# Attention values in two scaled float16 parts instead of three bfloat16 parts, from the second batch on

## The chip, the core and the metric

The kernel runs on one core of a Trainium2 chip. The metric is the device time of one execution in microseconds. Five engines work side by side: TensorE (PE in the profile, with its weight loads as PEld), VectorE (DVE), ScalarE (ACT), GpSimd (POOL) and SyncE (SP), which here issues every DMA.

## The reference

Inputs are q, k and v of shape (4, 8, 768, 64): 4 batches, 8 heads, 768 tokens, 64 numbers a head. The output of the attention goes through a mixture of four experts that all see every token.

```python
k_sum = k.reshape(B, H, nb, 32, D).max(axis=3)       # nb = 24 blocks
v_sum = v.reshape(B, H, nb, 32, D).mean(axis=3)
scores_l = scale * q @ k.T        # kept only where |i - j| < 16
scores_s = scale * q @ k_sum.T + log(32)
a = softmax(concat([scores_l, scores_s]))
attn = a @ concat([v, v_sum])     # (B, H, S, D) -> x of (3072, 512)
p = domain_probs / (domain_probs.sum(-1, keepdims=True) + 1e-9)
for e in range(4):
    h = np.maximum(x @ w1[e], 0.0)            # 512 -> 1024
    out += p[:, e:e+1] * (h @ w2[e])          # 1024 -> 512
```

## The kernel before

**Pieces.** The attention is cut into 64 pieces. Piece n handles batch n // 16, the 96 queries number (n // 2) % 8, and four heads (n % 2 says which four). For its 96 queries it needs 128 neighbouring keys (a window) and 24 block summaries. Pieces 0 to 7 are done by a separate function in the first 40 us (`first_tokens`); pieces 8 to 63 go through the steps below.

**Steps of a piece.** `load_piece` loads k (tile `kr`) and q with v (tile `qv`). `stage_a` splits them into parts of lower precision, since products are formed from parts whose sum is the full number: `ks` and `qs` as float32r parts for the scores, and v as three bfloat16 parts (`v12` holds the first two, `v3` the third), made by ACT, POOL, ACT and POOL in turn. `scores` forms the score matrix (PSUM tile `psc`), the maxima on DVE and the exponentials on ACT (tile `ms`). `probs` scales by the row sum (`rs`) and writes the weights as two float16 parts into tile `aw`; the weights of the 24 summaries are stored there as five blocks of 24 columns (`a5`: three copies of the high part, two of the rest). `transposed` turns `aw` by a DMA transpose into `awT`. `values` multiplies: for each of 4 heads, v1·hi, v1·lo, v2·hi, v2·lo, v3·hi and the summaries, thus 6 matmuls of 96 columns a head and 24 a piece, into PSUM tile `px`. Two heads at a time use the left and the right 64 columns of the array. `to_x` scales px away by 1/ASC; from piece 16 on it goes to DRAM (`xs`, `xd`) and comes back later as `xr`.

**Once per batch.** `setup_k` loads k in four chunks of 128x768 (`kch`) and takes block maxima. `setup_v` loads v likewise (`vch`), takes block sums, and `stack_v` and `split_v` make of them the summary operand `vs`: 4 transposes (`pvs`), a copy, and 8 instructions on DVE that split it into bfloat16 parts. All chunks share two buffers (tag "chunk"), so the third load waits until the first chunk has been reduced.

**The experts.** Tokens go through the experts in blocks of 384, the last six blocks in three pairs. The first product gives PSUM tiles `ph`, or `pha` to `phd` for the pairs (a seven-product scheme); `to_h` splits the result into `hh` and `hl`; the second product gives `po`, which DVE adds into `acc`. Weights arrive as `wr`, are split into high and low parts and are stored split in DRAM (`wd`, `wds`) for the later blocks.

**What sets the order.** The function writes a list `steps` of (place, step, piece), and `advance` puts steps between the matmuls of the experts by place. The setup of batch b stands two places (k) and half a place or one place (v) ahead of its first piece; a place is one piece. Up to the eighth place, the program order is kept; from there on a scheduler with a timeline of its own orders the instructions of each engine, apart from the chunk loads, which stay in program order. Every engine works its list in order, and SP's list is one queue: a DMA that must wait holds all DMAs behind it.

Of the kernel before, what the change touches and what calls it, by code (L numbers as in the profile page):

```python
# [21 lines left out]
QB = 96  # L22
# [40 lines left out]
def attn_moe(ctx: ExitStack, tc: tile.TileContext, qvL, qv0, v0L, kD, kT, vT, w1L, w2L, dpL, cst, out):  # L63
# [46 lines left out]
    def mixing():  # L110
        SP.dma_start(pw, dpL)
        s = const.tile([P, NT, 1], F32, name="dps")
        V.tensor_reduce(s, pw, axis=AX.X, op=ALU.add)
        V.tensor_scalar_add(s, s, EPS)
        V.reciprocal(s, s)
        V.tensor_tensor(pw, pw, s.broadcast_to([P, NT, E]), op=ALU.mult)


    per = 2 * (TB // QB)
    aw_bufs = {}  # L120

# [19 lines left out]
    def load_chunk(b, hp, ch, src):  # L141
        tc.keep_in_program_order(
            nc.sync.dma_start(ch, src[b, 2 * hp : 2 * hp + 2].rearrange("h d s -> (h d) s"))
        )
# [4 lines left out]
    def chunk(name):  # L149
        return sb.tile([P, S], F32, name=name, tag="chunk", bufs=CHUNKS)  # L150
# [17 lines left out]
    def setup_v(b):  # L168
# [4 lines left out]
            block_stats(ch, vsr, hp, ALU.add)  # L173
        stack_v(b, vsr)

    def stack_v(b, vsr):
        vs5 = sb.tile([P, G, 5, NB], F32, name=f"vs5_{b}", tag="chunk", bufs=CHUNKS)
        A.mul(vs5, vsr.rearrange("p h (o n) -> p h o n", o=1).broadcast_to([P, G, 5, NB]), 1.0 / BLK)
        pt = ps_av.tile([P, 512], F32, name=f"pvs{b}", tag="av")
        for hp in range(G):  # L180
            PE.transpose(
                pt[:NST, hp * P : (hp + 1) * P],
                vs5[:, hp].rearrange("p o n -> p (o n)"),
                ident,
            )
        v0 = sb.tile([NST, 512], F32, name=f"v0_{b}", tag="chunk", bufs=CHUNKS)
        A.copy(v0, pt[:NST, :])
        split_v(b, v0)

    def split_v(b, v0):  # L190
        b12 = sb.tile([NST, 2, 512], BF16, name=f"b12_{b}", tag="awT", bufs=2)
        b1, b2 = b12[:, 0, :], b12[:, 1, :]
        V.tensor_copy(b1, v0)
        V.tensor_tensor(v0, v0, b1, op=ALU.subtract)
        V.tensor_copy(b2, v0)
        V.tensor_tensor(v0, v0, b2, op=ALU.subtract)
        V.tensor_scalar_mul(b1, b1, gsel[0])
# [21 lines left out]
    def stage_a(n):  # L219
        b, i, g = n // 16, (n // 2) % NQ, n % 2  # L220
        h0 = g * G
        t = st[n]
        qr = t["qv"][:, 0 : G * QB].rearrange("p (h s) -> p h s", s=QB)
        vr = t["qv"][:, G * QB :].rearrange("p (h d) -> p h d", d=D)
        kr = t["kr"]
        PL.tensor_copy(kr[:, :, KW:KA], ksum[b][:, h0 : h0 + G, :])
        ks = []
        tag, bufs = ("x", NX) if spare_x(n) else ("kl", 2)
        for half in range(2):
            k2 = sb.tile([P, 2, 2, KA], F32R, name=f"ks{n}_{half}", tag=tag, bufs=bufs)  # L230
# [12 lines left out]
        PL.tensor_tensor(v3, vr, v12[:, :, 1, :], op=ALU.subtract)
        t.update(ks=ks, qs=qs, v=(v12, v3))
# [33 lines left out]
    def probs(n):  # L278
        ms, rs = st[n]["ms"], st[n]["rs"]
        aw = aw_of(n)  # L280
        V.tensor_scalar(rs, rs, EPS, 1.0 / ASC, op0=ALU.add, op1=ALU.mult)
        V.reciprocal(rs, rs)
        V.tensor_tensor(
            ms, ms, rs.rearrange("p (h o) -> p h o", o=1).broadcast_to([QB, G, KA]), op=ALU.mult
        )
        A.copy(aw[:, 0:G, :], ms[:, :, 0:KW])
        V.tensor_tensor(aw[:, G : 2 * G, :], ms[:, :, 0:KW], aw[:, 0:G, :], op=ALU.subtract)
        sm = ms[:, :, KW:KA]
        a5 = aw[:, 2 * G : 3 * G, 0:NST].rearrange("p h (o n) -> p h o n", n=NB)
        sm = sm.rearrange("p h (o n) -> p h o n", o=1)  # L290
        A.copy(a5[:, :, 0:3, :], sm.broadcast_to([QB, G, 3, NB]))
        V.tensor_tensor(
            a5[:, :, 3:5, :], sm.broadcast_to([QB, G, 2, NB]), a5[:, :, 0:2, :], op=ALU.subtract
        )
# [7 lines left out]
    def values(n):  # L302
        b, g = n // 16, n % 2
        t = st[n]
        awT, (v12, v3), vs = t["awT"], t["v"], vsum[b]
        if g == 0:
            t["bank"] = ps_av.tile([P, 512], F32, name=f"px{n}", tag="av")
        else:
            t["bank"] = st[n - 1]["bank"]
        px = t["px"] = t["bank"][:, g * 2 * QB : (g + 1) * 2 * QB].rearrange("p (c q) -> p c q", q=QB)  # L310
        for c in range(2):
            terms = []
            for j in (2 * c, 2 * c + 1):
                hi, lo, su = awT[:, j, :], awT[:, G + j, :], awT[:NST, 2 * G + j, :]
# [10 lines left out]
            for m in range(6):  # L325
                for o in range(2):
                    PE.matmul(px[o * D : (o + 1) * D, c, :], *terms[o][m], start=m == 0, stop=m == 5)

    def both_values(n):
        values(n - 1)  # L330
# [8 lines left out]
    def to_x(n):  # L339
        i = (n // 2) % NQ  # L340
        tb, ib = n // per, i % (TB // QB)
        pair = [st.pop(m)["px"] for m in (n - 1, n)]
        if tb < 2:
            if tb not in xT:
                xT[tb] = x_block(tb)
            parts = [[x[:, :, ib * QB : (ib + 1) * QB] for x in xT[tb][g]] for g in range(2)]
            for g in range(2):
                A.mul(parts[g][0], pair[g], 1.0 / ASC)
            for g in range(2):
                V.scalar_tensor_tensor(  # L350
                    parts[g][1], pair[g], 1.0 / ASC, parts[g][0].bitcast(F32), op0=ALU.mult, op1=ALU.subtract
                )
            return
        xs = sb.tile([P, 2, 2, QB], F32, name=f"xs{n}", tag="xt")
        A.mul(xs[:, 0], pair[0], 1.0 / ASC)
        A.mul(xs[:, 1], pair[1], 1.0 / ASC)
        if (tb // 2, ib) not in xraw:
            xraw[tb // 2, ib] = dram.tile([P, 4, 2, QB], F32, name=f"xd{tb // 2}_{ib}")
        SP.dma_start(xraw[tb // 2, ib][:, tb % 2 : 4 : 2], xs)
        written[tb // 2, ib] = written.get((tb // 2, ib), 0) + 2  # L360
# [685 lines left out]
```

## Time and profile before

| | us |
|---|---|
| median of 3 runs (1173.69 to 1174.64) | 1174.48 |
| the profiled execution | 1176.52 |
| its span, first to last instruction | 1174.7 |
| PE busy | 1150.5 (98%) |
| DVE busy | 631.4 (54%) |
| ACT busy | 541.2 (46%) |
| POOL busy | 468.5 (40%) |

The profiled execution took 1.8 us more than its span and 2.0 us more than the median of the runs. In the list of stretches, each engine stands with its busy time and the number of its instructions in brackets, followed by the clock that was granted to PE (1.00 is full), the busy share of the DMA engines, and the rate. In the chain of work that ended last, each row is start, length and what was done. A group row ends with its count, its busy time and the mean of one in ns, then the idle time ahead of it.

### The profile page before, as it was taken

The page shows a single profiled execution, that of the slowest core. Times are in us where ns is not written, and L with a number is a line of the kernel's source. Part 1 is how long each engine was busy: PE and PEld are TensorE (multiplying, and loading weights), DVE is VectorE, ACT ScalarE, POOL GpSimd, SP SyncE. Part 2 cuts the span into 40 slices and gives each one's busy share as a digit, 9 for nine tenths or more (in the row PEclk, how much of TensorE's full clock was granted, in tenths as well). Part 3 has the DMA queues.
Part 4 walks back from the last instruction along what each step waited for, and adds up shares of the span by engine and source line. Part 5 has one row for each costly group of instructions (what it writes and reads, how often), then busy time and mean ns, then how long its engine had stood idle before and what let it go on. Part 6 is the DMA issues. An engine that isn't in the chain of part 4 may idle for free.

```text
span 1174.7 us, 20612 instructions
## 1 busy us (share of the span) xinstructions
PE 1150.5 (98%) x7188; PEld 1021.0 (87%) x7188; DVE 631.4 (54%) x1519; ACT 541.2 (46%) x1586; POOL 468.5 (40%) x578
## 2 busy tenths in 40 slices
PE   9898899999979999999999999999999999999998
PEld 7787789998968989898898989889898998989896
DVE  6778775555796837558586543535354222323131
ACT  5678667655666736546375443434343211202020
POOL 2398677846786737547265122221202000000000
PEclk9999999999999999999999999999999999999999
DMA  6699787957996878789963859678571556566531
GB/s 240 227 281 321 225 250 218 305 118 215 307 251 182 272 228 263 225 277 288 320 196 102 255 149 289 202 213 284 141 205 61 159 156 212 165 197 189 163 98 54
DMA packets 202329, 249.66 MB, mean 213 GB/s; under 512 B 82672, under 2 KB 118512, under 8 KB 202224
## 3 DMA queue, kind: packets, MB, share of 16 engines
q1 hardware_dynamic: 202224, 248.34, 69.6%
q8 instruction: 57, 0.93, 0.3%
q14 instruction: 48, 0.39, 0.1%
HBM read 174.22 MB, written 57.15 MB: 197 GB/s over the span
## 4 chain that ended last, share of the span: by engine, by line
PE 85%; DMA 4%; DVE 4%; POOL 3%; ACT 2%; issue 1%; SPq 1%; POOLq 0%; DVEq 0%; ACTq 0%
PE po L75 42%; PE phb L75 13%; PE pha L75 9%; PE ph L75 5%; PE phd L75 4%; PE phc L75 4%; PE psc L75 4%; PE px L75 3%; DMA vch<-in_vT 1%; PE pav L75 1%; DMA wr<-in_w2L 1%; DMA kch<-in_kT 1%; DVE ms L75 1%; SPq L75 1%; ACT ms L75 1%
## 5 line engine op out<-in xcount | busy, mean ns | idle before, releaser
L75 PE MATMUL po<-w,hh 128*128 128x512 f32 x1536 | 480.5, 394 | 0.0
L75 PEld LDWEIGHTS po<-w,hh 128*128 128x128 f32 x1536 | 284.2, 188 | 61.0
L75 PE MATMUL po<-w,hl 128*128 128x512 f32 x768 | 302.8, 397 | 0.0
L75 PEld LDWEIGHTS po<-w,hl 128*128 128x128 f32 x768 | 144.4, 188 | 31.5
L75 POOL TENSOR_TENSOR ks<-kr,ks 128x304 fp32r<-128x304 f32 x112 | 99.7, 897 | 176.8 <-ACT ks L75 160.5
L75 DVE CUSTOM_DVE_ANT_0 ms<-psc,c_sb 96x152 f32<-96x152 f32 x256 | 69.2, 306 | 104.6 <-PE psc L75 103.4
L75 PE MATMUL phb<-xh_t,w1s 128*128 128x384 f32 x384 | 114.2, 338 | 0.1
L75 ACT ACTIVATE ms<-ms,nb 96x152 f32<-96x152 f32 x256 | 104.3, 415 | 16.5 <-DVE nb L75 15.6
L75 PE MATMUL pha<-xh,w 128*128 128x384 f32 x384 | 110.7, 335 | 0.0
L75 DVE SCALAR_TENSOR_TENSOR acc<-po,pw,acc 128x512 f32<-128x512 f32 x72 | 51.9, 746 | 108.8 <-PE po L75 108.8
L75 PE MATMUL ph<-xh,wh 128*128 128x384 f32 x256 | 88.0, 347 | 4.8 <-ACT wh L75 3.7
L75 PE MATMUL ph<-xl,wh 128*128 128x384 f32 x256 | 87.4, 341 | 2.3 <-DVE xl L75 2.3
L75 DVE TENSOR_TENSOR aw<-ms,aw 96x512 f16<-96x512 f32 x112 | 77.2, 723 | 21.5 <-ACT aw L75 21.3
L75 PE MATMUL ph<-xh,wl 128*128 128x384 f32 x256 | 87.1, 341 | 1.2 <-POOL wl L75 1.2
L75 ACT CAST ks<-kr 128x304 fp32r<-128x304 f32 x112 | 48.1, 445 | 80.4 <-PE psc L75 62.9
L75 POOL TENSOR_TENSOR wl<-wr,wh 128x512 fp32r<-128x512 f32 x44 | 62.6, 1425 | 45.0 <-ACT wh L75 44.9
L75 ACT CAST aw<-ms 96x512 f16<-96x512 f32 x112 | 53.3, 523 | 56.3 <-issue 37.8
L75 POOL TENSOR_TENSOR qv<-qv,v 128x256 f32<-128x256 f32 x56 | 40.8, 739 | 78.2 <-ACT v L75 78.0
L75 ACT CAST v<-qv 128x256 bf16<-128x256 f32 x112 | 44.5, 405 | 59.2 <-PE px L75 40.8
L75 PEld LDWEIGHTS phb<-xh_t,w1s 128*128 128x128 f32 x384 | 70.8, 188 | 1.0 <-ACT phb L75 0.2
L75 PEld LDWEIGHTS pha<-xh,w 128*128 128x128 f32 x384 | 70.5, 188 | 0.3
L75 PE MATMUL phb<-xl_t,w1s 128*128 128x384 f32 x192 | 64.3, 335 | 0.0
(122 smaller groups left out, 2169.3 us busy)
## 6 DMA issues: line engine op xcount, KB each, us to landing
w<-wd SPq DMA_DIRECT2D x80, 512.0 KB, 4.4
w1s<-wds SPq DMA_DIRECT2D x112, 256.0 KB, 3.5
w<-wd SPq DMA_DIRECT2D x84, 256.0 KB, 3.4
wr<-in_w1L SPq DMA_DIRECT2D x76, 256.0 KB, 4.3
qv<-in_qvL SPq DMA_DIRECT2D x56, 320.0 KB, 4.4
wd<-w SPq DMA_DIRECT2D x32, 512.0 KB, 4.3
wds<-w1s SPq DMA_DIRECT2D x64, 256.0 KB, 2.7
kr<-in_kD SPq DMA_DIRECT2D x56, 256.0 KB, 3.7
```

What stands on the lines that cost most here:

```text
L75: ins = getattr(self.engine, name)(*a, **kw)
```

## The change

For pieces 16 to 63, v is scaled by a power of two and split into two float16 parts: ACT writes the first (`v2[:, 0]`), DVE writes the rest in one instruction. `values` then needs v1·hi, v1·lo, v2·hi and the summaries: 4 matmuls a head, 16 a piece. The summary weights in `aw` take three blocks instead of five (N3 = 72 columns, not 120), `stack_v` splits the summaries by 4 DVE instructions instead of 8, and `to_x` undoes the scale. Batch 0 stays as it was.

The scale must be known before the first piece of a batch is split. A new step, `scan_v`, stands six places ahead of the batch: it loads the four chunks of v once more (`vm`), takes the largest magnitude of each partition on DVE, writes the 128 numbers to DRAM (`v1d`), reads them back to every partition (`v1e`), takes the maximum and makes the scale and its inverse by five small DVE instructions. The chunks use the same two buffers, and all six DMAs go through SP's queue.

```diff
+    def over_partitions(m, k, name):
+        room = dram.tile([P, k], F32, name=f"{name}d")
+        SP.dma_start(room, m)
+        every = sb.tile([P, P, k], F32, name=f"{name}e", tag="hs", bufs=2)
+        flat = room.rearrange("p k -> (p k)").rearrange("(o n) -> o n", o=1)
+        SP.dma_start(every.rearrange("p q k -> p (q k)"), flat.broadcast_to([P, P * k]))
+        return every
+
+    def scale_of(m, every, name):
+        V.tensor_reduce(m, every.rearrange("p q k -> p k q"), axis=AX.X, op=ALU.max)
+        s = const.tile([P, 2], F32, name=f"{name}s")
+        V.tensor_scalar(m, m, LEAST, MOST, op0=ALU.max, op1=ALU.min)
...
+    def scan_v(b):
+        top = sb.tile([P, G], F32, name=f"vt{b}", tag="vt")
+        for hp in range(H // 2):
+            ch = chunk(f"vm{b}_{hp}")
+            load_chunk(b, hp, ch, vT)
+            V.tensor_reduce(top[:, hp : hp + 1], ch, axis=AX.X, op=ALU.max, apply_absolute_value=True)
+        m = const.tile([P, 1], F32, name=f"vm{b}")
+        V.tensor_reduce(m, top, axis=AX.X, op=ALU.max)
+        v_scale[b] = scale_of(m, over_partitions(m, 1, f"v{b}"), f"v{b}")
...
-        v0 = sb.tile([NST, 512], F32, name=f"v0_{b}", tag="chunk", bufs=CHUNKS)
-        A.copy(v0, pt[:NST, :])
-        split_v(b, v0)
+        v0 = sb.tile([N3, 512], F32, name=f"v0_{b}", tag="chunk", bufs=CHUNKS)
+        A.activation(v0, pt[:N3, :], AF.Copy, scale=v_scale[b][0][:N3])
+        hi = sb.tile([N3, 512], F16, name=f"vh_{b}", tag="awT", bufs=2)
+        V.tensor_copy(hi, v0)
+        V.tensor_tensor(v0, v0, hi, op=ALU.subtract)
+        V.tensor_scalar_mul(hi, hi, no_low)
+        vs = sb.tile([N3, H, D], F16, name=f"vs{b}", tag="vs", bufs=2)
+        V.scalar_tensor_tensor(
+            vs.rearrange("p h d -> p (h d)"), v0, gsel[1][:N3], hi, op0=ALU.mult, op1=ALU.add
+        )
...
+        if b > 0:
+            v2 = sb.tile([P, 2, G, D], F16, name=f"v2_{n}", tag="v12", bufs=4)
+            scale = v_scale[b][0]
+            A.activation(v2[:, 0], vr, AF.Copy, scale=scale)
+            V.scalar_tensor_tensor(v2[:, 1], vr, scale, v2[:, 0], op0=ALU.mult, op1=ALU.subtract)
+            t.update(ks=ks, qs=qs, v=v2)
+            return
...
+        if n >= 2 * NQ:
+            a3 = aw[:, 2 * G : 3 * G, 0:N3].rearrange("p h (o n) -> p h o n", n=NB)
+            sm = sm.rearrange("p h (o n) -> p h o n", o=1)
+            A.copy(a3[:, :, 0:2, :], sm.broadcast_to([QB, G, 2, NB]))
+            V.tensor_tensor(a3[:, :, 2:3, :], sm, a3[:, :, 0:1, :], op=ALU.subtract)
+            return
...
+                if scaled:
+                    vh, vl = t["v"][:, 0, j, :], t["v"][:, 1, j, :]
+                    terms.append(((vh, hi), (vh, lo), (vl, hi), (vs[:, g * G + j, :], su)))
+                    continue
...
-        A.mul(xs[:, 0], pair[0], 1.0 / ASC)
-        A.mul(xs[:, 1], pair[1], 1.0 / ASC)
+        scale = v_scale[n // 16][1]
+        A.activation(xs[:, 0], pair[0], AF.Copy, scale=scale)
+        A.activation(xs[:, 1], pair[1], AF.Copy, scale=scale)
...
+        steps.append((k - 6.0, scan_v, b))
```

Because the scheduler orders anew, instructions move that the diff does not name. Two places matter below. The first is SP's queue while batch 1 is scanned, in the first block's experts: `wr11_7` and `wr21_7` are the eighth weight tiles of expert 1 (first and second product), `awT11` and `awT12` the transposes of pieces 11 and 12. Before:

```order
L75 DMA wr11_7_1564<-in_w1L 128x512
L75 DMA_TRANSPOSE awT11_1172<-aw1_887 128x12x96
L75 DMA kr15_1387<-in_kD 128x4x128
L75 DMA qv15_1388<-in_qvL 128x640
L75 DMA wd21_5_1520<-w21_5_1517 128x1024
L75 DMA wr21_7_1668<-in_w2L 128x512
L75 DMA kr16_1714<-in_kD 128x4x128
L75 DMA wr11_0_2081<-in_w1L 128x512
L75 DMA_TRANSPOSE awT12_1373<-aw0_746 128x12x96
```

The same place in SP's queue of the changed kernel, from the transpose of piece 11 on:

```order
L79 DMA_TRANSPOSE awT11_1200<-aw1_889 128x12x96
L79 DMA v1d_1139<-vm1_1137 128x1
L79 DMA_TRANSPOSE awT12_1401<-aw0_748 128x12x96
L79 DMA v1e_1141<-v1d_1139 128x128
L79 DMA kr15_1415<-in_kD 128x4x128
L79 DMA wd21_5_1548<-w21_5_1545 128x1024
L79 DMA wr21_6_1585<-in_w2L 128x512
L79 DMA wr11_7_1592<-in_w1L 128x512
L79 DMA wr21_7_1696<-in_w2L 128x512
```

The last weight tiles of expert 1 (`wr21_6`, `wr11_7`, `wr21_7`) stood around the transpose of piece 11; now they stand behind the scan's write `v1d`, the transpose of piece 12 and the scan's read `v1e`.

The second place is PE's list at the values of pieces 11 and 12, in the same stretch; `ph0_1_6` is the first product of block 0, expert 1, with weight tile 6. Before, behind the last matmul of piece 11:

```order
L75 LDWEIGHTS vs0_689
L75 MATMUL px10_1290<-awT11_1172,vs0_689 64x96
L75 MATMUL ph0_1_6_1528<-xh0_0_105,wl11_6_1525 128x384
L75 MATMUL ph0_1_6_1528<-xh0_0_105,wh11_6_1524 128x384
L75 MATMUL ph0_1_6_1528<-xl0_0_106,wh11_6_1524 128x384
L75 MATMUL ph0_1_6_1528<-xh0_0_105,wl11_6_1525 128x384
```

In the changed kernel, behind the last matmul of piece 11:

```order
L79 LDWEIGHTS vs0_691
L79 MATMUL px10_1318<-awT11_1200,vs0_691 64x96
L79 MATMUL ph0_1_6_1556<-xh0_0_106,wh11_6_1552 128x384
L79 MATMUL ph0_1_6_1556<-xl0_0_107,wh11_6_1552 128x384
L79 LDWEIGHTS v12_12_1185
L79 MATMUL px12_1647<-awT12_1401,v12_12_1185 64x96
L79 LDWEIGHTS v12_12_1185
```

The values of piece 12 came after the rest of `ph0_1_6`, after `ph0_1_7` and after 16 matmuls of `po`; now they follow piece 11 with two matmuls between.

More of the change, by code (lines that the diff above doesn't have):

```diff
@@ L12 @@
 F16 = mybir.dt.float16
+I32 = mybir.dt.int32
 AF = mybir.ActivationFunctionType
@@ L31 @@
 NST = 5 * NB
+N3 = 3 * NB
 SCALE = 1.0 / math.sqrt(D)
@@ L45 @@
 NW1 = 14
+TOP = 4.0
+LEAST, MOST = 2.0**-100, 2.0**100
 ASC = 32768.0
@@ L116, in mixing @@
         V.tensor_tensor(pw, pw, s.broadcast_to([P, NT, E]), op=ALU.mult)
+    def over_partitions(m, k, name):
[9 more added lines that the diff above has]
+        V.tensor_scalar(m, m, LEAST, MOST, op0=ALU.max, op1=ALU.min)
+        bits = m.bitcast(I32)
+        V.tensor_single_scalar(bits, bits, 0x7F800000, op=ALU.bitwise_and)
+        V.tensor_scalar_mul(s[:, 1:2], m, 1.0 / TOP / ASC)
+        V.tensor_scalar(s[:, 0:1].bitcast(I32), bits, -1.0, float(0x7F000000), op0=ALU.mult, op1=ALU.add)
+        V.tensor_scalar_mul(s[:, 0:1], s[:, 0:1], TOP)
+        return s[:, 0:1], s[:, 1:2]
+    v_scale = {}
+    no_low = const.tile([N3, 1], F32, name="no_low")
     per = 2 * (TB // QB)
@@ L174, in setup_v @@
         stack_v(b, vsr)
+    def scan_v(b):
[7 more added lines that the diff above has]
+        v_scale[b] = scale_of(m, over_partitions(m, 1, f"v{b}"), f"v{b}")
     def stack_v(b, vsr):
-        vs5 = sb.tile([P, G, 5, NB], F32, name=f"vs5_{b}", tag="chunk", bufs=CHUNKS)
-        A.mul(vs5, vsr.rearrange("p h (o n) -> p h o n", o=1).broadcast_to([P, G, 5, NB]), 1.0 / BLK)
+        vs3 = sb.tile([P, G, 3, NB], F32, name=f"vs3_{b}", tag="chunk", bufs=CHUNKS)
+        A.mul(vs3, vsr.rearrange("p h (o n) -> p h o n", o=1).broadcast_to([P, G, 3, NB]), 1.0 / BLK)
         pt = ps_av.tile([P, 512], F32, name=f"pvs{b}", tag="av")
@@ L181, in stack_v @@
             PE.transpose(
-                pt[:NST, hp * P : (hp + 1) * P],
-                vs5[:, hp].rearrange("p o n -> p (o n)"),
+                pt[:N3, hp * P : (hp + 1) * P],
+                vs3[:, hp].rearrange("p o n -> p (o n)"),
                 ident,
             )
-        v0 = sb.tile([NST, 512], F32, name=f"v0_{b}", tag="chunk", bufs=CHUNKS)
-        A.copy(v0, pt[:NST, :])
-        split_v(b, v0)
+        v0 = sb.tile([N3, 512], F32, name=f"v0_{b}", tag="chunk", bufs=CHUNKS)
[8 more added lines that the diff above has]
+        )
+        vsum[b] = vs
     def split_v(b, v0):
@@ L304, in values @@
         t = st[n]
-        awT, (v12, v3), vs = t["awT"], t["v"], vsum[b]
+        awT, vs, scaled = t["awT"], vsum[b], b > 0
+        if not scaled:
+            v12, v3 = t["v"]
         if g == 0:
@@ L313, in values @@
             for j in (2 * c, 2 * c + 1):
-                hi, lo, su = awT[:, j, :], awT[:, G + j, :], awT[:NST, 2 * G + j, :]
+                hi, lo, su = awT[:, j, :], awT[:, G + j, :], awT[: N3 if scaled else NST, 2 * G + j, :]
+                if scaled:
+                    vh, vl = t["v"][:, 0, j, :], t["v"][:, 1, j, :]
+                    terms.append(((vh, hi), (vh, lo), (vl, hi), (vs[:, g * G + j, :], su)))
+                    continue
                 terms.append(
@@ L324, in values @@
                 )
-            for m in range(6):
+            last = len(terms[0]) - 1
+            for m in range(last + 1):
                 for o in range(2):
-                    PE.matmul(px[o * D : (o + 1) * D, c, :], *terms[o][m], start=m == 0, stop=m == 5)
+                    PE.matmul(px[o * D : (o + 1) * D, c, :], *terms[o][m], start=m == 0, stop=m == last)
     def both_values(n):
@@ L948, in attn_moe @@
     mixing()
+    V.tensor_scalar(no_low, gsel[1][:N3], -1.0, 1.0, op0=ALU.mult, op1=ALU.add)
     advance(per)
```

## The prediction

> **What bounds the kernel now.** I read the page first, then the chain of work, then the stretches, and last the waits.
>
> ```profile
> span 1174.7 us, 20612 instructions
> ...
> PE 1150.5 (98%) x7188; PEld 1021.0 (87%) x7188; DVE 631.4 (54%) x1519; ACT 541.2 (46%) x1586; POOL 468.5 (40%) x578
> ...
> PE 85%; DMA 4%; DVE 4%; POOL 3%; ACT 2%; issue 1%; SPq 1%; POOLq 0%; DVEq 0%; ACTq 0%
> ```
>
> PE is the bound: it is busy for 98% of the span and makes up 85% of the chain. The other engines matter only where PE waits, so I ask where that is.
>
> ```profile
> core 0: us, PE busy (x) PEld busy (x) DVE busy (x) ACT busy (x) POOL busy (x), PEclk, DMA share, GB/s
> 90.00:130.00 40.00, 35.29 (x296) 29.94 (x296) 36.30 (x80) 28.97 (x88) 32.13 (x33) 1.00 0.97 265
> 130.00:165.00 35.00, 32.61 (x241) 29.99 (x237) 27.35 (x67) 22.18 (x65) 27.69 (x29) 0.95 0.79 236
> 165.00:280.00 115.00, 113.84 (x822) 102.29 (x821) 62.87 (x168) 73.65 (x223) 77.31 (x87) 1.00 0.75 216
> 280.00:350.00 70.00, 63.13 (x454) 57.58 (x454) 58.42 (x124) 43.10 (x132) 56.43 (x61) 0.98 0.96 282
> 380.00:900.00 520.00, 519.94 (x3271) 462.47 (x3271) 289.91 (x701) 252.04 (x762) 208.33 (x276) 1.00 0.73 223
> ```
>
> From 380 to 900 us PE does not pause. It lacks 4.7 us in 90 to 130, 2.4 in 130 to 165, 1.2 in 165 to 280 and 6.9 in 280 to 350. In the first and the fourth of these the DMA engines (0.97, 0.96) and DVE (36.3 of 40, 58.4 of 70) are nearly full. So the kernel has two kinds of time: dense stretches, in which a matmul less is time gained, and tight ones (90 to 130, the end of 280 to 350), in which DVE, POOL and DMA decide.
>
> **Term 1, the matmuls.** Each changed piece loses 8 of 24 matmuls: 48 pieces × 8 = 384. Their price is read from the chain, in which runs of values stand alone:
>
> ```profile
> 111.86 0.64 PE px L75 x24
> 270.06 1.16 PE px L75 x48
> ...
> L75 ACT ACTIVATE xs<-px x48: 319/324/367, 165.1 to 898.2; 128x192 f32<-128x192 f32 x48
> ```
>
> 48 matmuls take 1.16 us, 24.2 ns each; the 24 that distinguish the two rows take 0.52 us, 21.7 ns each. So 384 of them are 9.3 or 8.3 us; I take the middle, 8.8. The third row, the evacuation of exactly the changed pieces, says where they lie: from 165 to 898 us, in dense time but for the end of the fourth stretch. Nothing hides them, so the gain is whole: −8.8.
>
> **Term 2, the work moved between engines.** The prices, by group:
>
> ```profile
> L75 POOL TENSOR_TENSOR v<-qv,v 128x256 bf16<-128x256 f32 x56 | 41.8, 749 | 7.8 <-ACT v L75 6.8 <-PE phc L75 0.5
> L75 POOL TENSOR_TENSOR qv<-qv,v 128x256 f32<-128x256 f32 x56 | 40.8, 739 | 78.2 <-ACT v L75 78.0
> L75 ACT CAST v<-qv 128x256 bf16<-128x256 f32 x112 | 44.5, 405 | 59.2 <-PE px L75 40.8 <-POOL qv L75 13.5 <-DMA qv<-in_qvL 3.8
> L75 DVE TENSOR_TENSOR aw<-ms,aw 96x192 f16<-96x192 f32 x56 | 31.5, 562 | 0.0
> L75 DVE TENSOR_TENSOR w1s<-wr,w1s 128x256 fp32r<-128x256 f32 x48 | 28.2, 597 | 8.4 <-ACT w1s L75 8.3
> L75 DVE TENSOR_REDUCE vsr<-vch 128x24 f32<-128x768 f32 x12 | 11.4, 947 | 8.8 <-DMA vch<-in_vT 8.7
> ```
>
> POOL loses two instructions a piece: 48 × (739 + 749) = 71 us less. ACT loses one cast of two: 48 × 405 = 19 us less. DVE gains the split of v's rest, 128x256 with two operands in SBUF; the nearest row of that shape is 597 ns, so 28.7 us. Its `aw` rest shrinks from 192 to 96 columns; half of 562 ns is an estimate and saves 13.5 us. Three scans add 12 reductions of 947 ns, 11.4 us. Only the net on DVE, some 25 us on 631, loads an engine more. From 380 us on PE waits for nothing and DVE is busy for 290 of 520 us, so there it costs 0; that PE time is the cover. What is lost if the cover goes is the third rival below.
>
> **Term 3, the wait at 345 us.** The largest single pause of PE is here:
>
> ```profile
> 342.72 1.15 DVE aw L75
> ...
> 345.00 4.91 DMA awT<-aw
> ...
> 349.95 1.17 PE px L75 x24
> ```
>
> ```profile
> 344.00:348.00 4.00, 0.40 (x20) 0.30 (x13) 3.25 (x10) 2.08 (x7) 3.92 (x5) 0.88 0.41 135
> 348.00:352.00 4.00, 2.05 (x29) 1.93 (x29) 3.14 (x6) 1.20 (x3) 0.80 (x2) 0.50 0.97 254
> 352.00:356.00 4.00, 4.00 (x14) 3.20 (x14) 2.60 (x4) 3.19 (x11) 3.82 (x7) 0.77 1.00 303
> 349.95 0.61 PE L75 MATMUL px<-awT,v 128*64 128x96 f16 x10 [5.55 <-DMA awT<-aw]
> ```
>
> PE waits 5.55 us for the transpose of a piece whose `aw` DVE finished late, after the setup of batch 2. Then the clock is 0.50 for 4 us and 0.77 for 4 more, a further 2.9 us. The setup's split on DVE changes:
>
> ```profile
> L75 DVE TENSOR_TENSOR v<-v,b 120x512 f32<-120x512 f32 x8 | 7.1, 882 | 0.1
> L75 DVE CAST b<-v 120x512 bf16<-120x512 f32 x8 | 4.6, 573 | 2.0 <-ACT v L75 2.0
> L75 DVE SCALAR_TENSOR_TENSOR b<-b,c_sb 120x512 bf16<-120x512 bf16 x4 | 4.0, 1005 | 0.0
> ```
>
> Eight instructions become four; one cast (573), one subtraction (882) and one combination (1005) fall away, 2.5 us. Two pieces' `aw` rests save 0.3 us each, two new splits cost 0.6 each: net −1.9 us ahead of the late `aw`. I take −2. The bounds are −8.5 (wait and slow clock gone) and +0.9 (PE comes earlier by the matmuls of two or three pairs and waits them out, with DVE no sooner).
>
> **Term 4, the scan of batch 1.** It starts where SP stands at 85 us, just ahead of the tightest stretch. Its nearest relative is batch 1's own load of k:
>
> ```profile
> 91.30 1.11 SPq L75 DMA_DIRECT2D wr<-in_w1L  x1
> 93.47 0.42 SPq L75 DMA_DIRECT2D wr<-in_w2L  x1
> 94.22 0.73 SPq L75 DMA_DIRECT2D wr<-in_w1L  x1
> ...
> 107.29 0.92 SPq L143 DMA_DIRECT2D kch<-in_kT  x2
> 114.32 1.19 SPq L143 DMA_DIRECT2D kch<-in_kT  x2
> ...
> 113.36 1.79 DVE L75 TENSOR_REDUCE ksr<-kch 128x24 f32<-128x768 f32 x2
> xd<-xs SPq DMA_DIRECT2D x24, 192.0 KB, 2.8
> 103.39 0.44 PE L75 MATMUL ph<-xh,wl 128*128 128x384 f32 x1 [1.19 <-POOL wl L75]
> ```
>
> A second pair of chunks was issued 7.0 us after the first, when DVE had reduced it. Carried over: first pair at 86, second at 93, reduced by 101, `v1d` then, its landing 2.8 us later (the smallest store shown, 192 KB; 512 B may be quicker), `v1e` at 104. SP holds everything behind these waits: the second-product weights 6, issued at 93.47, and the first-product weights 7, issued at 94.22, would go at 105, some 11 us later. PE used the tile before these, issued at 91.30, at 103.39, after a wait of 1.19 us, so 12 us passed between issue and use; with part of that slack PE would reach weights 7 about 4 us too soon. Against it, PE then has its work in a heap and loses less of the 4.7 + 2.4 us that it lacks up to 165 us. Bounds: −1 (the heap repays it) and +10.5 (the delay falls on PE whole). I take +3, nearer the row with 12 us of slack.
>
> The scans of batches 2 and 3 stand near 200 and 420 us, where PE lacks 1.2 us in 115 and nothing in 520: +0.5 together, between 0 and 2.
>
> **The sum.** −8.8 − 2 + 3 + 0.5 = −7.3 us. The span goes from 1174.7 to 1167.4, the profiled execution from 1176.5 to 1169.2, the median from 1174.5 to 1167.2. The profiled execution stood 2.0 us above the median, which I carry along. The least that a measurement here can tell from no change is about 0.2%, 2.3 us.
>
> **Rivals.**
>
> A: the wait at 345 us disappears. For it: POOL and DVE hinder each other. `rs`, 96x4, is the same instruction in both DVE rows:
>
> ```profile
> 122.09 0.17 DVE L75 TENSOR_SCALAR rs<-rs 96x4 f32<-96x4 f32 x1 [0.23 <-ACT ms L75]
> 122.91 0.92 POOL L75 TENSOR_TENSOR qv<-qv,v 128x256 f32<-128x256 f32 x1 [1.62 <-ACT v L75]
> 331.28 0.83 POOL L75 TENSOR_TENSOR ks<-kr,ks 128x304 fp32r<-128x304 f32 x1
> 331.30 0.83 DVE L75 TENSOR_SCALAR rs<-rs 96x4 f32<-96x4 f32 x1
> ```
>
> At 122.09 POOL was idle (until 122.91, for 1.62 us) and `rs` took 0.17 us; at 331.30 it ran as long as POOL's instruction beside it, 0.83 us. With 71 us of POOL gone, DVE's other instructions shorten too, and the −2 becomes −8.5: 1174.5 − 8.8 − 8.5 + 3.5 = 1160.7. Against it: the chain also runs through DMA loads that stay. The Trainium skill ("SBUF — State Buffer", Who interferes with whom) says that a VectorE instruction in a two-port mode, or with two SBUF inputs against a GpSimd read, shares a port pair with GpSimd, and that the later one blocks fully. The two rows agree; by that rule alone the forecast's −2 is too small. The same skill ("TensorE: Matmul & The Clock Gate", Part 1) lets the clock halve after some 3.4 us of idleness; the 5.55 us and the 0.50 agree, and by it a wait cut below that would return the 2.9 us as well.
>
> B, the other side: SP's hold for `v1d` and `v1e`. If the 11 us delay of weights 7 reaches PE nearly whole (10.5), the pause is longer than the 5.55 us that was followed by a slow clock, so 2.9 us come on top: −8.8 − 2 + 0.5 + 13.4 = +3.1, 1177.6. It decides from a loss of 10.3 us on. For it: the DMA share of 0.97; against it: the 12 us between issue and use.
>
> C: the new DVE split waits in order behind ACT's, which waited for `px` to free its buffers (40.8 us in the ACT row above). What stands behind it on DVE are `hl` and the sums that release PSUM, for which PE waits next. If this costs 0.3 us in each of 24 pairs, 7 us go: 1174. Against it: ACT, upstream of `hl`, was held the same way and PE did not pause.
>
> **How the numbers follow.** Forecast 0.56 (1163 to 1172), A 0.20 (1157 to 1163), C 0.12 (1172 to 1176), B 0.12 (1175 to 1180). Faster is forecast and A, 0.76; same is C, 0.12; slower is B, 0.12. The range 1159 to 1175 leaves out B and the lowest part of A, about 0.18.
>
> **What would show it.** Right: `px` runs of 32 in about 0.8 us; PE busy without pause from 380 us on; PE's time short of the stretch in 90 to 130 up by some 3 us; the wait at 345 us down by about 2. Wrong: a pause at piece 12 or at weights 7 of more than 6 us with the clock down (B), no pause near 345 (A), or PE waits after 380 us on DVE (C).

## The result, and the profile after

The changed kernel is slower: a median of 1192.46 us over 5 runs against 1174.64 for the kernel before, a ratio of 1.0138 with a 95% interval from 1.0115 to 1.0162. The forecast was 1167.2. The profiled execution took 1192.89 us.

The head of the page of the changed kernel and the first line of its chain:

```profile
span 1191.1 us, 19798 instructions
...
PE 1152.6 (97%) x6804; PEld 1019.6 (86%) x6804; DVE 642.2 (54%) x1592; ACT 530.6 (45%) x1538; POOL 396.2 (33%) x482
...
PE 71%; DMA 5%; DVE 2%; POOL 1%; ACT 1%; issue 1%; SPq 0%; POOLq 0%; DVEq 0%; ACTq 0%
```

PE has 384 matmuls fewer (7188 to 6804) and yet more busy time (1150.5 to 1152.6), and its share of the chain fell from 85% to 71%. The stretches of the changed kernel say where:

```profile
core 0: us, PE busy (x) PEld busy (x) DVE busy (x) ACT busy (x) POOL busy (x), PEclk, DMA share, GB/s
90.00:130.00 40.00, 27.41 (x177) 23.09 (x176) 30.46 (x76) 23.04 (x70) 22.40 (x22) 0.74 0.88 247
130.00:165.00 35.00, 34.74 (x253) 31.14 (x252) 25.77 (x63) 20.88 (x61) 19.96 (x22) 1.00 0.92 243
165.00:280.00 115.00, 106.08 (x705) 95.55 (x705) 69.36 (x188) 67.47 (x202) 62.13 (x64) 0.97 0.89 231
280.00:350.00 70.00, 70.00 (x449) 63.31 (x449) 45.59 (x114) 39.95 (x117) 42.38 (x44) 1.00 0.82 249
350.00:380.00 30.00, 23.31 (x138) 18.32 (x137) 26.40 (x64) 21.58 (x72) 23.54 (x30) 0.89 0.88 247
380.00:900.00 520.00, 519.82 (x3087) 461.99 (x3086) 300.68 (x747) 249.63 (x744) 174.46 (x228) 1.00 0.77 230
```

In 90 to 130 us PE lacks 12.6 us instead of 4.7, and its clock is 0.74 instead of 1.00; in 165 to 280 it lacks 8.9 instead of 1.2. From 380 us on it is as dense as before. These are the places of the scans of batches 1 and 2; the third, near 500 us, leaves no mark.

**A common mileage.** The same clock time means different work in two kernels. So I counted, along PE's timeline, the experts' matmuls (384 and 512 columns; 5,088 are recorded in each kernel, in almost the same order) and noted when the k-th ended, in us from the start of the span. A place k in this count is called a mark below.

| k | before | changed | no trip | no scan | row for trip | best |
|---|---|---|---|---|---|---|
| 200 | 89.4 | 90.3 | 90.4 | 89.4 | 90.9 | 90.4 |
| 400 | 147.3 | 160.4 | 155.3 | 149.7 | 157.4 | 153.8 |
| 700 | 217.9 | 231.9 | 227.8 | 218.6 | 227.0 | 223.6 |
| 900 | 261.4 | 282.8 | 269.3 | 262.9 | 268.5 | 265.1 |
| 1300 | 363.2 | 384.8 | 369.0 | 363.6 | 367.9 | 359.8 |
| 3000 | 736.1 | 754.5 | 738.0 | 732.3 | 736.4 | 729.0 |
| 5088 | 1171.0 | 1187.3 | 1171.0 | 1165.9 | 1169.3 | 1161.9 |

The columns from the fourth on belong to experiments below: the changed kernel without its trip, without its scan, with the trip's write as one row, and the best complete version. The changed kernel loses 12.2 us between marks 200 and 400 and 7.4 between 700 and 900, 21.6 in all by mark 1300; from there to the end it wins back 5.3.

**The first loss.** SP's list of the changed kernel while batch 1 is scanned (start, length, DMA), and DVE at the same time (in brackets the idle time ahead of a row and what ended it):

```profile
103.96 0.33 SPq L79 DMA_DIRECT2D v1d<-vm  x1
107.24 1.28 SPq L79 DMA_TRANSPOSE awT<-aw  x1
112.08 0.33 SPq L79 DMA_DIRECT2D v1e<-v1d  x1
...
113.49 0.42 SPq L79 DMA_DIRECT2D wr<-in_w2L  x1
114.00 0.76 SPq L79 DMA_DIRECT2D wr<-in_w1L  x1
```

```profile
117.55 0.29 DVE L79 TENSOR_REDUCE vm<-v1e 128x1 f32<-128x128 f32 x1 [5.92 <-DMA v1e<-v1d]
```

The DMA groups of the changed kernel (count, size, median us from issue to landing) say why `v1e` waits until 112.08:

```profile
xd<-xs SPq DMA_DIRECT2D x24, 192.0 KB, 3.2
v1e<-v1d SPq DMA_DIRECT2D x1, 64.0 KB, 5.4
v1d<-vm SPq DMA_DIRECT2D x1, 0.5 KB, 8.1
v2d<-vm SPq DMA_DIRECT2D x1, 0.5 KB, 10.6
v3d<-vm SPq DMA_DIRECT2D x1, 0.5 KB, 10.5
```

Half a kilobyte takes 8.1 to 10.6 us to land, three times as long as 192 KB. Until it has landed SP issues nothing but one transpose, which itself waited for its `aw` until 107.24, and in parts of this time the DMA engines run empty (0 GB/s from 106 to 108 us and from 110 to 114). This is the stretch from 104 to 116 us in the changed kernel, then the same stretch before, and then in the changed kernel without its trip to DRAM and back (the first experiment below):

```profile
104.00:116.00 12.00, 6.42 (x63) 5.44 (x62) 7.15 (x23) 8.37 (x29) 6.03 (x6) 0.64 0.37 46
```

```profile
104.00:116.00 12.00, 12.00 (x84) 10.49 (x83) 11.86 (x27) 7.72 (x26) 9.75 (x10) 1.00 1.09 297
```

```profile
104.00:116.00 12.00, 8.43 (x79) 7.00 (x78) 11.66 (x39) 10.75 (x34) 6.64 (x7) 0.72 0.84 225
```

In the tightest place of the kernel the transfers fall from 297 to 46 GB/s for 12 us. PE lacks 5.6 of these 12 us and runs at 0.64 of its clock for the rest. The third row says how much of this is the trip's: without it the rate is 225 GB/s, but PE still lacks 3.6 us, at a clock of 0.72. There, too, SP stands at a transpose, which the new order has moved ahead of the weight loads:

```profile
102.72 0.53 SPq L79 DMA_DIRECT2D kr<-in_kD  x1
107.73 1.28 SPq L79 DMA_TRANSPOSE awT<-aw  x1
...
110.22 0.76 SPq L79 DMA_DIRECT2D wr<-in_w1L  x1
```

The last row is first-product weights 7. They went at 94.22 before, go at 110.22 without the trip and at 114.00 with it.

PE's longest pause in the stretch from 90 to 130 us runs through DVE's list. DVE stands 5.92 us at the reduction of `v1e`, and the next `ms` behind it; ACT's `aw` needs that `ms`, ACT's `ks` stands behind `aw`, and PE waits 4.47 us:

```profile
119.64 0.95 ACT L79 CAST aw<-ms 96x512 f16<-96x512 f32 x2 [6.68 <-issue]
121.02 0.44 ACT L79 CAST ks<-kr 128x304 fp32r<-128x304 f32 x1
121.56 0.41 PE L79 MATMUL psc<-ks,qs 128*96 128x152 f32 x1 [4.47 <-issue]
```

The profile names no releaser for the two waits ("issue"); that they are `ms` and `ks` is inferred from the times and the names.

**The second loss.** At batch 2, too, DVE stands. Its list in the changed kernel, and the row of PE that waited for it:

```profile
248.15 0.55 DVE L79 SCALAR_TENSOR_TENSOR hl<-ph,hh 128x384 fp32r<-128x384 f32 x1
257.75 0.29 DVE L79 TENSOR_REDUCE vm<-v2e 128x1 f32<-128x128 f32 x1 [9.05 <-DMA v2e<-v2d]
...
258.76 0.55 DVE L79 SCALAR_TENSOR_TENSOR hl<-ph,hh 128x384 fp32r<-128x384 f32 x1
```

```profile
259.37 0.69 PE L79 MATMUL ph<-xh,wh 128*128 128x384 f32 x1 [6.87 <-DVE hl L79]
```

The reduction of what was read back stands in DVE's list ahead of the next `hl`. It waits 9.05 us, `hl` behind it too, and PE 6.87 us for `hl`.

### The profile page after: what moved, and what is told of

It reads as the page before. It is cut to its first block, busy times and chain, and to the rows that moved or that the text cites. A ratio compares the mean times of both kernels' runs of the same rounds, so it can differ in the third digit from the quotient of the medians.

```text
span 1191.1 us, 19798 instructions
## 1 busy us (share of the span) xinstructions
PE 1152.6 (97%) x6804; PEld 1019.6 (86%) x6804; DVE 642.2 (54%) x1592; ACT 530.6 (45%) x1538; POOL 396.2 (33%) x482
## 4 chain that ended last, share of the span: by engine, by line
PE 71%; DMA 5%; DVE 2%; POOL 1%; ACT 1%; issue 1%; SPq 0%; POOLq 0%; DVEq 0%; ACTq 0%
PE po L79 37%; PE phb L79 13%; PE pha L79 8%; PE phd L79 4%; PE phc L79 4%; PE psc L79 2%; PE px L79 1%; PE ph L79 1%; DMA wr<-in_w2L 1%; DMA v2d<-vm 1%; DMA v3d<-vm 1%; DMA wr<-in_w1L 1%; DMA v2e<-v2d 1%; DMA awT<-aw 0%; ACT ms L79 0%
## 5 line engine op out<-in xcount | busy, mean ns | idle before, releaser
L79 PE MATMUL ph<-xh,wh 128*128 128x384 f32 x256 | 90.3, 357 | 13.1 <-DVE hl L79 7.4
L79 ACT CAST aw<-ms 96x512 f16<-96x512 f32 x112 | 49.6, 489 | 70.8 <-issue 45.9
L79 DVE TENSOR_TENSOR aw<-ms,aw 96x512 f16<-96x512 f32 x112 | 64.2, 610 | 19.1 <-ACT aw L79 19.1
L79 PEld LDWEIGHTS psc<-ks,qs 128*96 128x96 f32 x448 | 53.6, 166 | 19.0 <-POOL qs L79 7.9
L79 PE MATMUL psc<-ks,qs 128*96 128x152 f32 x448 | 57.5, 252 | 11.3 <-POOL qs L79 6.9
L79 POOL TENSOR_TENSOR qs<-qv,qs 64x384 fp32r<-64x384 f32 x56 | 58.3, 1041 | 22.9 <-issue 6.4
```

The costliest lines, as they stand in the source:

```text
L79: ins = getattr(self.engine, name)(*a, **kw)
```

## The experiments

All ratios are to the kernel before, run beside it on the same chip, with 95% intervals; a ratio is not always that of the two medians, and where that matters both are given. My theory was the trip: the write to DRAM and the read back hold SP's queue and DVE's list. Its rivals were the scan's own loads and reductions, and the new forms and order of DVE's and ACT's work.

### Leaving the trip out

```diff
-        v_scale[b] = scale_of(m, over_partitions(m, 1, f"v{b}"), f"v{b}")
+        v_scale[b] = scale_of(m, None, f"v{b}")    # no reduction over partitions
```

> The changed kernel, but each partition takes the scale from its own largest value: the scan's loads, its four reductions and the arithmetic of the scale stay, the write of 128 x 4 bytes, its read back to all partitions (64 KB) and DVE's reduction over 128 columns are left out (the values are therefore scaled by 128 different numbers). The trip theory: the three trips (8.1 + 5.4, 10.6 + 6.1, 10.5 + 3.8 us of landing) hold SP's queue and DVE's list, and cost nearly all that the change lost over its matmul gain, so this run stands at 1163 to 1171 us, with the window from 90 to 130 us back above 33 us of PE and no DVE wait for v1e, v2e, v3e. Rival one (the scan's own 1.5 MB of loads and reductions in the tight stretch is the loss): it stays above 1184. Rival two (the new order and form of DVE's and ACT's work is the loss): it stays above 1184 too.

Measured: 1176.66 us, 0.9993 (0.9974 to 1.0012). The trip costs 1.45% in the changed kernel, some 17 us, as much as the whole loss (1.38%). In the table the column "no trip" is 5.1 us ahead of the changed kernel at mark 400, 13.5 at 900, 15.8 at 1300 and 16.3 at the end: trips 1 and 2 cost nearly everything, trip 3 at most 0.5 us. From 90 to 130 us PE is busy for 33.55 us again, as expected. But 1163 to 1171 was missed by 5.7 us: something else costs as well.

### Leaving the scan out as well

```diff
-        top = sb.tile([P, G], F32, name=f"vt{b}", tag="vt")
-        for hp in range(H // 2):
...
-        v_scale[b] = scale_of(m, over_partitions(m, 1, f"v{b}"), f"v{b}")
+        s = const.tile([P, 2], F32, name=f"v{b}s")    # a constant scale
...
+        v_scale[b] = s[:, 0:1], s[:, 1:2]
```

> The changed kernel without the scan and the trip: the scale of every batch is a constant, set once. What is left is the smaller number of matmuls for the values, the two float16 parts and the new work of ACT and DVE. The trip theory: faster than the kernel before by most of the matmul term, 1162 to 1168 us. Rival one (scan): the same 1162 to 1168, so only the distance to the run with the scan but no trip tells these two apart. Rival two (new forms on DVE and ACT): 1180 or more, no gain left.

Measured: 1170.32 us, 0.9918 (0.9888 to 0.9948): 0.82% faster than before, 9.6 us at 1174.5 (6.6 us by the medians, 5.1 by the end of the table), and 2 us above the range. So the smaller number of matmuls does pay, and whatever the new forms on DVE and ACT cost is less than that gain. Between this run and the one without the trip lie 0.75%, some 9 us (6.3 by the medians, 5.1 by the table): the scan itself. By the table that cost arises before mark 700 (9.2 us there, 5.4 at mark 1300).

One thing goes with the scan that is neither a load nor a reduction. In this run the values of pieces 10, 11 and 12 stand in PE's list as in the kernel before, after 215, 242 and 280 of the experts' matmuls; with the scan, with or without its trip, they stand after 228, 240 and 242. So what this run takes away is the scan and the new order together.

### The loads of the scan alone

```diff
+        for hp in range(H // 2):               # into the kernel with a constant scale
+            ch = chunk(f"vm{b}_{hp}")
+            load_chunk(b, hp, ch, vT)
```

> The run without scan and trip (constant scale), with the scan's twelve loads of 384 KB put back at their places, but not its reductions; what is loaded is not read. The scan cost 6 us (1176.7 against 1170.3). If that is the loads, in the stretch where the DMA engines are full: 1174 to 1178. If it is the reductions and what they delay on DVE: 1168 to 1172.

Measured: 1173.26 us, 0.9960 (0.9943 to 0.9976). It falls just between the two expectations' numbers: of the scan's 0.75%, the loads make about 0.4 and the reductions and what stands behind them about 0.3. With these intervals the halves are not better known than to some 0.3; that both have a part is not shown. Nor does this run part the loads from the new order: with them the values of pieces 10 to 12 are back after 228, 240 and 242, and PE is busy for 8.54 of the 12 us from 104 to 116, as without the trip (8.43), though nothing is reduced. No run has the scan's own loads in the old order.

### The maximum over the partitions on the chip

```diff
+    def scale_v(b):
+        pt = ps_av.tile([P, 512], F32, name=f"pvm{b}", tag="av")
+        PE.matmul(pt[:, 0:P], m.broadcast_to([P, P]), ident, start=True, stop=True)
+        every = pt[:, 0:P].rearrange("p (q k) -> p q k", k=1)
+        v_scale[b] = scale_of(m, every, f"v{b}")
```

> The changed kernel with the maximum over the partitions found on the chip: one matmul turns the column of 128 maxima into 128 rows of it in PSUM, DVE reduces that, and nothing goes through DRAM; it is done two pieces after the scan. The output's computation is complete. The trip theory: within 3 us of the run that has the scan and no trip, 1164 to 1172 us, and faster than the kernel before. Rival one (the scan itself): above 1184. Rival two: above 1184.

Measured: 1179.51 us, 1.0004 (0.9986 to 1.0022), 2.9 us above the run without any trip. The full computation without the trip is back at the time before (2.6 us above it by the medians), but not below it; my range was again too low by the scan's price.

### The trip alone, in the kernel before

```diff
+    def trip(b):
+        ms = st[2 * per * b - 6]["ms"]
+        room = dram.tile([QB, 1], F32, name=f"v{b}d")
...
+        SP.dma_start(room, ms[:, 0, 0:1])
+        SP.dma_start(every.rearrange("p q k -> p (q k)"), flat.broadcast_to([P, QB]))
+        V.tensor_reduce(most, every.rearrange("p q k -> p k q"), axis=AX.X, op=ALU.max)
```

> The kernel before with three trips added and nothing else: 96 values of 4 bytes, one from each partition, are written to DRAM, read back to all partitions (48 KB) and reduced on DVE, at the places of the order where the changed kernel has its own; the result is not used. The trip theory: 8 to 20 us slower than the kernel before, 1183 to 1195, with landings of 8 to 11 us for the write and 4 to 6 for the read. Rival one (the scan itself): 0 to 4 us slower, 1174 to 1179. Rival two: 0 to 4 us slower as well.

Measured: 1188.59 us, 1.0079 (1.0050 to 1.0108), some 9 us (11.6 by the medians), as the trip theory said. In the changed kernel the trips cost 1.45%; why they cost more there isn't shown. The landings of this run:

```profile
v1d<-ms SPq DMA_DIRECT2D x1, 0.4 KB, 8.9
v2d<-ms SPq DMA_DIRECT2D x1, 0.4 KB, 7.7
v3d<-ms SPq DMA_DIRECT2D x1, 0.4 KB, 9.6
```

### One row in place of 96 writes

```diff
-        SP.dma_start(room, ms[:, 0, 0:1])
+        SP.dma_start(flat, ms[0:1, 0, 0:QB])
```

> The kernel before with three trips at the same places as in the run of the trip alone, but the 96 values of 4 bytes are written as one row of 384 bytes from one partition; the read back to all partitions and DVE's reduction stay. In the run of the trip alone the write landed after 8.9, 7.7 and 9.6 us and the kernel was 0.8% (9 us) slower. If it is the many small writes that are slow: the write lands in 2 to 4 us and the kernel loses 2 to 6 us (1179 to 1183 beside 1177). If the write waits behind the other transfers in flight whatever its shape: it lands in 7 to 10 us again and the loss stays at 8 to 11 us.

Measured: 1178.62 us, 1.0011 (0.9998 to 1.0023). The same number of bytes by the same queue at the same step costs 1 us (1.6 by the medians) and not 9, less than the 2 to 6 expected. The profile gives this write no landing time, but SP's list bounds it, since the read waits for the write. At batch 2:

```profile
248.95 0.26 SPq L75 DMA_DIRECT2D v2d<-ms  x1
249.33 0.39 SPq L75 DMA_DIRECT2D kr<-in_kD  x1
250.40 0.33 SPq L75 DMA_DIRECT2D v2e<-v2d  x1
```

1.45 us after the write's issue the read goes out. At batches 1 and 3 it goes out after 4.3 and 3.5 us, with other DMAs between that had waits of their own, so these are upper bounds. The profile of this run counts 330 DMA packets fewer than that of the trip alone. So it is the shape, one number from each partition, and not the bytes or the full queues. The two runs are not alike in all: with the slow write the scheduler put the summaries of batch 1 (`pvs`) after 360 of the experts' matmuls, here after 418. At mark 400 the run of the trip alone is 10.8 us behind the kernel before, this one 3.1; of the 7.7 us between them 5.0 arise between marks 300 and 400, where the orders differ.

### The trip without DVE's reduction

```diff
-        V.tensor_reduce(most, every.rearrange("p q k -> p k q"), axis=AX.X, op=ALU.max)
```

> The kernel before with three trips, the 96 writes of 4 bytes and the read back to all partitions, but without DVE's reduction, so that nothing on DVE waits for the read. SP theory (the loss is SP's queue, which stands for 7 to 9 us between write and read while loads wait behind it): the loss stays near that of the run with the reduction, 7 to 11 us (1184 to 1188 beside 1177). DVE theory (the loss is DVE's list, which stood 6.2, 9.3 and 9.5 us behind the reduction): 0 to 3 us remain (1177 to 1180).

Measured: 1184.00 us, 1.0057 (1.0039 to 1.0076). Most of the loss stays without any wait on DVE, but not all, and the mileage shows that the places differ. At mark 400 this run is 11.9 us behind the kernel before, with the reduction 10.8; from mark 850 to 900 it takes 11.5 us, as before (11.5), and with the reduction 17.7. So with the trip put into the kernel before, at batch 1 it is SP's queue, at batch 2 DVE's list, and at batch 3 neither. In the changed kernel DVE's list has a part at batch 1 too, by PE's pause of 4.47 us.

### Mending only the write in the changed kernel

```diff
+        PE.transpose(pt[:1, 0:P], m, ident)
+        row = sb.tile([1, P], F32, name=f"{name}w", tag="hs", bufs=2)
+        V.tensor_copy(row, pt[:1, 0:P])
-        SP.dma_start(room, m)
+        SP.dma_start(room.rearrange("p k -> (p k)").rearrange("(o n) -> o n", o=1), row)
```

> The changed kernel with one part of its trip mended: PE turns the column of 128 maxima into a row on one partition, DVE copies it out of PSUM, and it is written to DRAM as one row of 512 bytes; the read back to all partitions and DVE's reduction stay where they were. If it is the 128 writes of 4 bytes whose landing costs the time: the write lands in 2 to 4 us, and the time comes down from 1192 to within 5 us of the run without any trip, 1175 to 1182 beside 1177. If the round trip costs the same whatever its shape: 1188 or more.

Measured: 1179.54 us, 1.0026 (1.0011 to 1.0040). Of the trip's 1.45%, 1.1 are gone by this one edit; PE's list is almost that of the changed kernel, with the values of piece 12 again after 242, so the new order alone does not make the trip's cost. SP's list at batches 1 and 2:

```profile
106.14 0.30 SPq L79 DMA_DIRECT2D v1d<-v1w  x1
107.04 1.29 SPq L79 DMA_TRANSPOSE awT<-aw  x1
108.43 0.53 SPq L79 DMA_DIRECT2D v1e<-v1d  x1
...
245.22 1.20 SPq L79 DMA_DIRECT2D v2d<-v2w  x1
...
247.76 0.35 SPq L79 DMA_DIRECT2D v2e<-v2d  x1
```

From write to read 2.3 and 2.5 us pass instead of 8.1 and 10.6. (The profiled execution of this kernel was its fastest, 1175.43, so its column in the table flatters it by 4 us.)

### Without the scan's own loads

The block sums need the same four chunks. Four versions make one set of loads serve both and take the maximum over the partitions by the matmul. The first keeps bfloat16 for batch 1:

```diff
+            block_stats(ch, vsr, hp, ALU.add)
             V.tensor_reduce(top[:, hp : hp + 1], ch, axis=AX.X, op=ALU.max, apply_absolute_value=True)
...
+        if b == 1:
+            steps.append((k - 0.5, setup_v, b))
+        else:
+            steps += [(k - 6.0, scan_v, b), (k - 4.0, scale_v, b), (k - 1.0, sums_v, b)]
```

> The new form of the values for batches 2 and 3 alone; batch 1 uses three bfloat16 parts as in the kernel before. The scan has no loads of its own: the four loads that the block sums need are made six pieces ahead, and sums and maxima are taken from them; the maximum over the partitions comes by one matmul and a reduction. By the matmuls: 256 fewer, 5.9 us. If the first batch's scan stretch was the place where the scan cost its time (in the run with the scan and no trip PE had lost 10 us more than before by 217 us, and nothing more after it): 1166 to 1171 beside 1177, 0.5 to 0.9% faster. If the scan costs as much at every batch: 1174 to 1178, no gain.

Measured: 1174.57 us, 0.9978 (0.9964 to 0.9991); 2.6 us of the 5.9 arrive. That is short of the first answer (0.5 to 0.9%) and, at the edge of the second one's range, a little more than its "no gain". What takes the rest I didn't settle.

For batch 1 too, the loads ahead of the keys:

```diff
+        early = (2.6, 1.6) if b == 1 else (6.0, 4.0)
+        steps += [(k - early[0], scan_v, b), (k - early[1], scale_v, b), ...]
```

> As the run with batches 2 and 3, and batch 1 in the new form too: its four loads for sums and maxima come just ahead of the loads for the keys, 2.6 pieces before the batch, instead of twice. By the matmuls: 384 fewer, 8.8 us. If it was the scan's extra loads that cost time in the stretch from 90 to 165 us: 1163 to 1169 beside 1177, and at least as fast as the run with two batches. If it is the reductions and the early place: 1170 to 1178, slower than the run with two batches.

Measured: 1172.92 us, 0.9961 (0.9947 to 0.9975). It fits neither answer: the time lies in the second one's range, but the run is not slower than that with two batches. The third and the fourth only change `early` for batch 1, first to (1.6, 0.9), then to (3.4, 2.2):

> As the run with all three batches in the new form and no loads of the scan's own, but for batch 1 the four loads of the values come after those of the keys (1.6 pieces ahead of the batch, near where the kernel before has them) and not ahead of them. In the run with the values ahead of the keys PE lost 9 us more than before between 120 and 146 us, waiting for ks on ACT (4.0 us) and for the sums' turn (2.9 us). If those waits came from the keys' loads being late: 1163 to 1169 beside 1177, the best of all. If they come from the new order as such: 1171 to 1175 again.

Measured: 1172.26 us, 0.9956 (0.9940 to 0.9973), no better than (2.6, 1.6), and in the range of the second answer. PE's waits of this run from 125 to 165 us:

```profile
PE pvm L79 <- DVE vm L79: 7.2, 1, 7.2
```

Put late, the maximum's own matmul stands in PE's list and waits for DVE. The waits of the run before, for `ks` and the sums, are gone, and this one has taken their place.

> As the run with all three batches in the new form and no loads of the scan's own, with batch 1's four loads for sums and maxima still earlier: 3.4 pieces ahead of the batch, so that they stand 8 places earlier in SP's queue and the keys' loads 0 to 6 places earlier. In the run with 2.6 pieces PE lost 9 us more than before between 120 and 146 us (waits for ks on ACT, 4.0 us, and for the sums' turn, 2.9), in the run with the values behind the keys it waited 7.2 us for the maximum's own matmul. If both stalls are a matter of where the four loads stand: 1164 to 1169 beside 1177. If some stall of that size comes wherever the loads are put, since the stretch from 90 to 165 us has no room: 1171 to 1176.

Measured: 1168.94 us, 0.9939 (0.9918 to 0.9960), the lowest of the complete versions, ahead of both kernels, and near the run with no scan at all. It lies at the upper end of the first answer's range. Its interval overlaps those of the two versions before it, so the times alone don't set it apart from them; the trace shows what differs. The stretches that the change had broken, in this run:

```profile
90.00:130.00 40.00, 35.69 (x258) 29.85 (x257) 36.73 (x94) 26.86 (x84) 22.28 (x23) 0.91 1.05 298
130.00:165.00 35.00, 32.00 (x207) 28.77 (x206) 24.81 (x59) 23.15 (x66) 25.72 (x30) 0.90 0.64 175
165.00:280.00 115.00, 114.73 (x786) 102.47 (x786) 74.17 (x200) 70.21 (x207) 60.49 (x63) 1.00 0.79 230
```

No wait for the maximum or for the sums is left there; PE's longest from 90 to 165 us is 1.3 us. By this trace both stalls were a matter of place. Why this place is the right one stays open: the keys' loads did not come much sooner, the last one at 123.11 us against 124.95 with (2.6, 1.6).

## Why the prediction was wrong, step by step

**Term 4 failed, first by its landing time.** I took 2.8 us for the write of `v1d`, from "the smallest store shown, 192 KB", and added that 512 B may be quicker. It took 8.1 us, and 10.6 and 10.5 at the other scans. I sized a transfer by its bytes when what counted was its shape. The chain ahead of it held: `v1d` went at 103.96 (forecast 101), but `v1e` at 112.08 (forecast 104) and the first-product weights 7 at 114.00 (forecast 105).

The landing is not the whole of it, since without the trip these weights still went only at 110.22. The term was +3, with a bound of +10.5; between marks 200 and 400 the changed kernel lost 12.2 us. Of these, 5.2 go with the trip, 4.6 more with the rest of the scan, and 2.4 are left without any scan. The bound itself was nearly right, so I chose the wrong end of it: the slack of 12 us that I leaned on was one weight tile's, in a stretch that I had called tight.

**The scans of batches 2 and 3, +0.5 together.** Batch 2's trip alone costs 9.4 us between marks 700 and 900 (no trip 41.5 us, changed 50.9). The step that failed is "where PE lacks 1.2 us in 115": I took PE's small idle time for room. It only says that nobody stood in PE's way before; it doesn't say how long DVE or SP may stand. I had followed SP's hold and overlooked the same wait on DVE's in-order list, where `hl` is queued behind the reduction. For batch 3, a price near 0 was right.

**Priced only as SP's hold:** the scan beside the trip, 0.75% by the ratios. I counted the 11.4 us of reductions into DVE's total, and not into the tight stretch. The chunks' own traffic there, and the new order of pieces 10 to 12, have no term at all. Which of the three takes how much stays open.

**Term 1 was right.** A run of 32 matmuls of values in the changed kernel, from its first row to the row behind it:

```profile
871.38 0.32 PE L79 MATMUL px<-awT,v 128*64 128x96 f16 x6
...
872.05 0.21 PE L79 MATMUL px<-awT,vs 72*64 72x96 f16 x2
872.19 0.57 PE L79 MATMUL psc<-ks,qs 128*96 128x152 f32 x4
```

0.81 us, where 48 took 1.16: 0.35 us for each of 24 pairs, 8.4 us against the 8.8 forecast. It arrives in the dense time, as said: behind mark 1300 the changed kernel has 480 matmuls of values, the kernel before 720, and it takes 5.3 us less there (5.5 with no scan), 22 ns for each of the 240.

**Term 2 was right in what counts.** POOL's busy time fell by 72.3 us (forecast 71), ACT's by 10.6 (forecast 19) and DVE's rose by 10.8 (forecast 25). What ACT lacks is the scale as a number per partition, which I had left out: 48 casts of v take some 505 ns instead of 405, and 48 evacuations of `px` 408 instead of 324, 8.8 us in all. On DVE some unchanged instructions became shorter, the 56 `aw` of 96x512 from 883 to 804 ns and the 56 `rs` from 593 to 548; that is the way rival A pointed, but no run shows the cause. The run with no scan gained 9.6 us (6.6 by the medians), where terms 1 and 2 make 8.8, so the moved work takes little or none of it, and rival C, a wait for the new split from 380 us on, did not come: PE is busy for 519.82 of 520 us.

**Term 3: the wait moved.** The pause of 5.55 us at 345 us is gone, but two others stand 20 us later. PE's timeline of the changed kernel:

```profile
367.90 0.31 PE L79 MATMUL psc<-ks,qs 128*96 128x152 f32 x1 [2.88 <-POOL qs L79]
370.59 0.45 PE L79 MATMUL px<-awT,v 128*64 128x96 f16 x6 [2.37 <-DMA awT<-aw]
```

From mark 900 to 1300 the kernel before takes 101.8 us, the changed one 102.0 and the one without the trip 99.7. Of term 1's matmuls 64 fall there, 1.4 us. So instead of −2 the term was about +1.6 in the changed kernel and −0.7 without the trip, and rival A's −8.5 did not come. The 2.9 us of slow clock in rivals A and B were also too many, since they count idle time: 2.05 us busy at 0.50 and 4.00 at 0.77 lose 1.9. That changes neither outcome.

**Rival B** named the mechanism, SP's hold for `v1d` and `v1e`, and got 0.12. It was priced at +13.4 us for batch 1, near to the 12.2 that came there, but less than half of that went with the trip. That the same happens once more at batch 2, through DVE, took most of the time beyond its 1177.6.

## What to carry to other kernels

Size a DMA by its pieces as well as by its bytes: a column of one number per partition took 8 to 10 us to land here, a row of as many bytes at most 1.45 to 4.3, and a wait for it in a queue stops everything behind it, on the engine that issues the read and on the engine that uses it. To reduce over partitions, turn the column with a matmul on the chip, or at least write it as one row. An engine without idle time tells nothing of how long its suppliers may stand. Where a scheduler orders anew, look for the new order as a cost of its own. And ask of each new wait what is queued behind it on its own engine, and whether data that is loaded anyway could serve.

## What the runs showed of the hardware

The write of 128 values of 4 bytes, one from each partition, landed in 8.1 to 10.6 us, of 96 values in 7.7 to 10.1, while one row of 384 or 512 bytes let its reader go 1.45 to 4.3 us after its issue (six trips in two runs; the longest two have other waits in them). The Trainium skill ("DMA: Bandwidth & Descriptors", Anatomy of one DMA — SWDGE (gpsimd) path) fits a DMA that GpSimd issues by about 2.0 us and its bytes. If that held on SP's queue too, 512 B would, by estimate, take 2.0 us in either shape; the row's bounds are of that size, the column's landing is not, and the measurement decides. Whether the time goes into the single writes or into their confirmations isn't shown.

The chain of work isn't a bill. In the changed kernel it runs through the third trip:

```profile
499.09 10.48 DMA v3d<-vm
509.59 3.78 DMA v3e<-v3d
```

These 14.3 us are 1.2% of the span, and by the mileage they cost at most 0.5 us.

The scale as a number per partition made ACT's evacuation of `px` slower, 408 ns in the median against 324 with a constant. The Trainium skill ("ScalarE: Activation LUTs", What ACT_TABLE_LOAD costs) gives about 93 ns for each such operand; the 84 ns measured come near it.
